# A four-layer model on one core: rows turned by transposing DMA, queries projected with keys and values

## The chip, the cores and the metric

The kernel runs on one core of a Trainium2 chip. A core has five engines with instruction streams of their own: TensorE (PE in the profile, its weight loads PEld), VectorE (DVE), ScalarE (ACT), GpSimd (POOL) and SyncE (SP). Transfers go through 16 DMA engines that they share. A transfer is issued by an engine's queue, here nearly always SP's, and a queue issues in order: an issue that waits for something holds up all those behind it. Matmul results land in PSUM, eight banks of 2 KB per partition; the other data live in SBUF.

The metric is the device time of one execution in microseconds.

## What is computed

The input is 2048 tokens of width 640 in bfloat16. Four layers follow each other, A B A B, each of the form `x = x + f(layernorm(x))`, with the same weights for both A layers and for both B layers.

Layer A is attention in four segments of 512 tokens, with 32 heads of width 20, and a linear memory carried over the segments. Per head and segment:

```
logits = q @ k.T * scale + causal mask;  a_dot = softmax(logits) @ v
a_mem  = phi(q) @ M / (phi(q) @ z + 1e-6)      # phi(t) = t + 1 for t > 0, else exp(t)
o      = g * a_mem + (1 - g) * a_dot           # g = sigmoid(beta)
M += phi(k).T @ v;   z += sum of phi(k)
```

and the heads, side by side again, are multiplied by `wo`.

Layer B works through 64 segments of 32 tokens, with 32 heads of width 128. Each segment is put behind 8 memory rows, projected to queries, keys and values, and attended with a mask; the 8 memory rows of a segment's output are the memory of the next segment. So the 64 steps of B form one chain.

## The kernel before

**Layer A.** The heads are taken in groups of four: eight groups per segment, 32 in a layer (`NGR`), numbered g. A loop over g runs two groups longer than that, since a group's work is spread over several turns: the projections for g + 1, the scores of g, the second pass over the scores for a group one to two turns back, and the product with the values for g - 2. Each turn has four slots (`half` and `ph`). In each slot PE first visits score tiles, then works off a list of other items:

- Visits: S tiles are scores of queries against keys, from which DVE takes the negative maximum of each row (`s_max`, tile a_nm). T tiles are the same product turned round, with the maximum already in the queries (tile a_q, from `q_with_max`), which ACT passes through exp into a_PT; POOL then clears what lies above the diagonal.
- Items (`SLOTS`): QP (`proj_q`: queries, already turned, width on partitions), KV0 and KV1 (`proj_kv`: keys and values in natural layout, tokens on partitions, half a segment each), KT (`k_turn`: keys turned by PE), Q2 (`q_with_max`), NUM (`state_num`: the memory's share), UP (`state_up`: the memory's update), PV, and from the finished segment before otps (`out_stage_a`: the attention rows of 128 tokens turned by PE, copied by ACT to a_oT) and YP0, YP1 (`out_stage_b`: the product with `wo`, in two halves, to which DVE adds the residual a_xr into a_xnew).
- `seg_step` loads, normalises (`seg_norm`) and turns (`seg_tr`: five PE transposes, an ACT copy to a_xnT) the rows of the next segment, at the turns and slots in `TPS`.

S and T tiles share three PSUM buffers of two banks (`psx`); all items share two buffers of one bank (`pg`), so an item must wait until the tile of the item two before it has been copied out.

PE runs in the order of the program. For ACT, DVE and POOL `KeyOrder` sorts the instructions: each has a kind, and its place is that of its slot (`K.base`) plus the lag of its kind in `A_LAGS`, in slots. So a smaller lag puts an instruction earlier on its engine, and a step that moves to another slot moves its places too. DMA issues stand in SP's queue in the order that the compiler's planner gives them.

At the end of the layer the last segment's rows are turned by PE (`last_turns`) and written out; there the normalising of layer B's first rows already begins. While the first A layer runs, the weights of B are loaded piece by piece (`side_loads`), and the padded weights of A are kept in memory (`keep_padded`) for the second A layer.

**Layer B.** A step s projects its own 32 columns with the weights as moving operand (`thin_mm`: b_Ka, b_Kb, b_Qa, b_Qb, b_Va, b_Vb), turns the results (`transp4`), takes scores, softmax and the product with the values (b_OTP), and multiplies by the output weights (b_OPS). What concerns the 24 first tokens of a segment is written at once (`store_head`); the 8 last tokens come out of the following step's memory rows and are collected in b_OTdef for four segments, multiplied later in four pieces (`od_chunk`, b_OPSd) and written by `od_end` and `tail_dma`. On the last step the columns of the step after it are zeros. When the loop is over, four pieces, an `od_end` and two stores are left.

**Joints.** Where layer B ends and A begins, A's first rows (a_xt), its weights (a_wq_pad, a_wkv) and B's last stores stand in SP's queue together.

Of the kernel before, what the change touches and what calls it, by code (L numbers as in the profile page):

```python
# [18 lines left out]
F32 = mybir.dt.float32  # L19
# [18 lines left out]
def alloc_consts(tc, ctx):  # L38
# [7 lines left out]
    C.pad = cp.tile([128, 2, 12], BF16, name="c_pad")  # L46
# [10 lines left out]
def build_consts(nc, tc, C):  # L57
    with ExitStack() as tctx:
# [13 lines left out]
        for i in range(2):  # L72
            nc.vector.tensor_copy(C.negu[:, i, :], neguf[:])
# [125 lines left out]
class AWeights:  # L199
# [3 lines left out]
A_LAGS = {"dsel": 0.5, "EK": -1.0, "EKm": 1.05, "EQ": 2.0, "Kn": 0.5, "MZ": 3.5, "MZb": 3.5, "NM1": -0.3, "On": 3.2, "adn":  # L203
# [6 lines left out]
def build_gates(nc, pool, W, A_beta):  # L210
    bb = pool.tile([128, 32], BF16, name="a_beta_bf")
    with nc.allow_non_contiguous_dma(reason="beta bcast"):
        nc.sync.dma_start(bb[:], A_beta.partition_broadcast(128))
    e = pool.tile([128, 32], F32, name="a_beta_e")
# [9 lines left out]
def load_A_weights(nc, W, A_wq, A_wk, A_wv, A_wo, padded, stage):  # L224

    first = not padded
    if first:
        for nm, src in (("wq", A_wq), ("wk", A_wk), ("wv", A_wv)):
            nc.sync.dma_start(stage[nm], src.rearrange("(c p) n -> p c n", p=128))
    else:  # L230
        nc.sync.dma_start(W.wq[:].rearrange("p c h s -> p (c h s)"), padded["wq"])
        nc.sync.dma_start(W.wkv[:].rearrange("p c g n -> p (c g n)"), padded["wkv"])
    nc.sync.dma_start(W.wo[:], A_wo.rearrange("(c p) n -> p c n", p=128))
    if first:
        K = yield
        nc.gpsimd.memset(W.wq[:, :, :, 20:32], 0.0)
        cast = K("cast").vector
        cast.tensor_copy(W.wq[:, :, :, 0:20], stage["wq"].rearrange("p c (h d) -> p c h d", d=20))
        for i, nm in enumerate(("wk", "wv")):
            cast.tensor_copy(W.wkv[:, :, :, 80 * i:80 * i + 80], stage[nm].rearrange("p c (g n) -> p c g n", n=80))  # L240
        yield


def keep_padded(nc, tc, W, padded):
    for nm, pad, n in (("wq", W.wq, 1024), ("wkv", W.wkv, 1280)):
        padded[nm] = tc.dram_tile([128, NCH * n], BF16, name=f"a_{nm}_home")
        nc.sync.dma_start(padded[nm], pad[:].rearrange("p c h s -> p (c h s)"))


def layer_A(nc, tc, C, W, x_src, x_dst, src_is_bf16, nseg=4, out_bf16=False, xb_dst=None, load_w=None, side_loads=None):  # L250
# [7 lines left out]
    with ExitStack() as ctx:  # L258
# [4 lines left out]
        W.wq = pw.tile([128, NCH, 32, 32], BF16, name="a_wq_pad")  # L263
        W.wkv = pw.tile([128, NCH, 8, 160], BF16, name="a_wkv")
# [6 lines left out]
        qp3 = pool("a_q3", 3)  # L271
# [18 lines left out]
        MZ32 = ste.tile([128, 8, 128], F32, name="a_MZ32")  # L290
        nc.vector.memset(MZ32[:], 0.0)
        MZb = stm.tile([128, 8, 128], BF16, name="a_MZb")
        vaug = [stm.tile([128, 4, 4, 32], BF16, name=f"a_vaug{i}") for i in range(4)]
        Kn = [stm.tile([128, 4, 4, 32], BF16, name=f"a_Kn{i}") for i in range(2)]
        phik = [ste.tile([128, 4, 4, 32], BF16, name=f"a_phik{i}") for i in range(2)]
        NM = [stm.tile([128, 4, 4, 32], BF16, name=f"a_NM{i}") for i in range(2)]

        def pads(i, eng):
            for on, dst, k in ((i < 2, Kn, 0), (True, vaug, 1)):
                if on:  # L300
                    src = C.pad[:, k, :].unsqueeze(1).unsqueeze(1).to_broadcast([128, 4, 4, 12])
                    (eng.copy if eng is nc.scalar else eng.tensor_copy)(dst[i][:, :, :, 20:32], src)

        nc.vector.tensor_scalar(out=MZ32[:].rearrange("p g (j e) -> p g j e", e=32)[:, :, :, 20],
                                in0=C.identb[:].rearrange("p (j e) -> p j e", e=32)[:, :, 20].unsqueeze(1).to_broadcast([128, 8, 4]),
                                scalar1=1e-6, scalar2=None, op0=ALU.mult)
# [20 lines left out]
        def seg_norm(n_, tt):  # L327
# [4 lines left out]
            for i in range(2):  # L332
                K("st").vector.bn_stats(out=stats[:, i, :], in_=xt[:, 320 * i:320 * i + 320])
# [9 lines left out]
        def seg_tr(n_, tt):  # L343
# [3 lines left out]
            xn = d["xn"][tt]  # L347
            tps = (pg if n_ else psx).tile([128, NCH, 128], BF16, name="a_tps", tag="pg" if n_ else "x")
# [4 lines left out]
        def out_stage_a(n_, tt):  # L353
# [6 lines left out]
            tps = pg.tile([128, NCH, 128], BF16, name="a_otps", tag="pg")  # L360
            for c in range(NCH):
                nc.tensor.transpose(tps[:, c, :], d["Onat"][:, tt, 128 * c:128 * c + 128], C.identb[:])
            K("oT").scalar.copy(oT[:], tps[:])

        def out_stage_b(n_, tt, halves=(0, 1)):
# [3 lines left out]
            if xr is None:  # L369
                xr = wkl.tile([128, D], BF16 if src_is_bf16 else F32, name="a_xr")  # L370
                nc.sync.dma_start(xr[:], x_src[r0:r0 + 128, :])
# [14 lines left out]
            xnb = w1l.tile([128, D], BF16, name="a_xnb")  # L386
            if n_ == nseg - 1:
                nc.scalar.copy(xnb[:], xnew[:])
            else:
                K("xnb").gpsimd.tensor_copy(xnb[:], xnew[:])  # L390
            nc.sync.dma_start(xb_dst[r0:r0 + 128, :], xnb[:])
# [3 lines left out]
        def proj_q(g):  # L395
            n, G = divmod(g, 8)
            s_ = GS[g] = {}
            xnT = SEG[n]["xnT"]
            wqG = W.wq[:, :, 4 * G:4 * G + 4, :].rearrange("p c h s -> p c (h s)")
            QP = pg.tile([128, 512], F32, name="a_QP", tag="pg")  # L400
            for c in range(NCH):
                nc.tensor.matmul(QP[:], lhsT=wqG[:, c, :], rhs=xnT[:, c, :], start=(c == 0), stop=(c == NCH - 1))
            qT = qp3.tile([128, 512], BF16, name="a_qT")
            K("qT").scalar.copy(qT[:], QP[:])
            s_["qT"] = qT
            if n >= 1:
                EQ = w1.tile([128, 512], BF16, name="a_EQ")
                K("EQ").scalar.activation(out=EQ[:], in_=qT[:], func=ACT.Exp)
                rq = w1.tile([128, 512], BF16, name="a_rq")
                K("rq").vector.tensor_scalar(out=rq[:], in0=qT[:], scalar1=0.0, scalar2=None, op0=ALU.max)  # L410
# [3 lines left out]

        def proj_kv(g, hf):
            n, G = divmod(g, 8)
            xnT = SEG[n]["xnT"]
            KV = pg.tile([128, 2, 160], F32, name="a_KV", tag="pg")
            for t2 in range(2):
                tt = 2 * hf + t2  # L420
                for c in range(NCH):
                    nc.tensor.matmul(KV[:, t2, :], lhsT=xnT[:, c, 128 * tt:128 * tt + 128], rhs=W.wkv[:, c, G, :],
                                     start=(c == 0), stop=(c == NCH - 1))
            for kd, dst, o in (("Kn", Kn[g % 2], 0), ("va", vaug[g % 4], 80)):
                K(kd).scalar.copy(dst[:, 2 * hf:2 * hf + 2, :, 0:20], KV[:, :, o:o + 80].rearrange("p t (j s) -> p t j s", s=20))
            GS[g]["va"] = vaug[g % 4]

        def k_turn(g):
            KT_ = pg.tile([128, 4, 128], BF16, name="a_KT", tag="pg")
            for tt in range(4):  # L430
                nc.tensor.transpose(KT_[:, tt, :], Kn[g % 2][:, tt, :, :].rearrange("p j s -> p (j s)"), C.identb[:])
            kT = qp4.tile([128, 512], BF16, name="a_kT")
# [956 lines left out]
```

## Time and profile before

| | us |
|---|---|
| median of 3 runs (2574.44 to 2577.28) | 2575.98 |
| the profiled execution | 2574.74 |
| its span | 2573.0 |

| engine | busy us | share of the span |
|---|---|---|
| PE | 2486.0 | 97% |
| PEld | 1639.1 | 64% |
| DVE | 1675.5 | 65% |
| ACT | 1519.1 | 59% |
| POOL | 696.2 | 27% |

The granted TensorE clock is 0.998 of full speed. The A layers lie at about 20 to 340 and 1300 to 1625 us of the span, the B layers between and behind them. PE is busy throughout; DVE and ACT are nearly full in the A layers and about half full in B. So the averages over the span are of little use, and the readings below are by stretch.

In a row of the timeline the first number is the start, the second the time from the first start to the last end of the merged instructions; since an engine overlaps an instruction with the next, what one costs is better read from its start to the start of the next. In a row of the chain of work the second number is only the part that lies on the chain. A row of waits has the total, the number and the longest.

### The profile page before, as it was taken

What the parts mean: (1) busy time and instruction counts of PE and PEld (TensorE: products, weight loads), DVE (VectorE), ACT (ScalarE), POOL (GpSimd) and SP (SyncE); (2) the same over time, 40 slices, a digit from 0 to 9 for tenths busy, and PEclk for the clock granted to TensorE, in tenths of its full rate; (3) what the DMA queues carried; (4) which work ended last, traced back from release to release, by engine and by line L of the source; (5) the groups of instructions that cost most, each with busy time, mean ns of one, the idle gap of its engine ahead of it and who ended that gap; (6) DMA issues with size and microseconds to landing.
All of it is one profiled execution on the core that took longest, in us unless ns stands there. A gap on an engine that the chain in (4) does not pass through costs nothing.

```text
span 2573.0 us, 139432 instructions
## 1 busy us (share of the span) xinstructions
PE 2486.0 (97%) x62088; PEld 1639.1 (64%) x62088; DVE 1675.5 (65%) x4597; ACT 1519.1 (59%) x3430; POOL 696.2 (27%) x1471
## 2 busy tenths in 40 slices
PE   7999999999999999999989999999999999999998
PEld 5666576666666666666655665766666666666665
DVE  8999845565556556555579998455655655555555
ACT  6999945555555545444369999445554555555443
POOL 5677621111111111111146776111111111111110
PEclk9999999999999999999999999999999999999999
DMA  4122372222222222121220212721212122111111
GB/s 158 46 85 78 91 239 45 50 48 44 51 45 48 46 50 46 39 39 29 63 84 17 68 53 86 233 47 43 45 41 50 42 45 47 42 42 34 38 26 21
DMA packets 325308, 157.18 MB, mean 61 GB/s; under 512 B 244960, under 2 KB 309600, under 8 KB 322912
## 3 DMA queue, kind: packets, MB, share of 16 engines
q1 hardware_dynamic: 324704, 148.26, 22.1%
q8 instruction: 485, 7.95, 1.3%
q14 instruction: 119, 0.97, 0.1%
HBM read 96.46 MB, written 51.71 MB: 58 GB/s over the span
## 4 chain that ended last, share of the span: by engine, by line
PE 78%; DVE 10%; ACT 8%; issue 2%; DMA 1%; POOL 1%; SPq 0%; ACTq 0%; DVEq 0%; POOLq 0%
PE b_OPS L110 11%; PE b_tail L110 6%; PE b_Ka L110 5%; PE b_Kb L110 5%; PE b_Qa L110 5%; PE b_Qb L110 5%; PE b_Va L110 5%; PE b_Vb L110 4%; DVE a_nm L139 4%; PE b_SP L110 4%; ACT a_PT L139 4%; PE b_vtail L110 3%; PE b_OPSd L110 3%; PE b_OTP L110 3%; PE a_S L110 2%
## 5 line engine op out<-in xcount | busy, mean ns | idle before, releaser
L110 PEld LDWEIGHTS <-b_HX 128*32 128x32 bf16 x15360 | 427.8, 96 | 331.3 <-issue 1.3
L110 POOL TENSOR_TENSOR b_Pn<-b_E,b_rs 128x200 bf16<-128x200 bf16 x128 | 78.0, 609 | 1332.7 <-PE b_Vb L110 1016.9
L139 DVE TENSOR_REDUCE a_nm<-a_S 128x2 f32<-128x512 f32 (+3 forms) x512 | 395.0, 816 | 53.1 <-PE a_S L110 38.1
L139 ACT ACTIVATE a_PT<-a_T 128x1024 bf16<-128x1024 f32 (+1 forms) x384 | 345.8, 904 | 28.3 <-PE a_T L110 21.0
L110 PE MATMUL b_OPS<-b_wo,b_OTsb 128*32 128x320 bf16 x8192 | 303.1, 300 | 1.6 <-issue 0.5
L110 PEld LDWEIGHTS <-b_OTsb 128*32 128x32 bf16 x8192 | 205.7, 96 | 76.3 <-DVE b_OTsb L110 3.3
L139 POOL TENSOR_SCALAR_AFFINE_SELECT a_PT<-a_PT 128x256 bf16<-128x256 bf16 x380 | 188.5, 501 | 154.7 <-ACT a_PT L139 153.4
L110 DVE CAST b_HX<-b_MT 128x8 bf16<-128x8 f32 x372 | 63.6, 172 | 234.0 <-PE b_MT L110 228.3
L110 ACT CAST b_msb<-b_OPS 128x64 bf16<-128x64 f32 x378 | 69.5, 256 | 223.7 <-PE b_OPS L110 223.6
L110 ACT CAST b_kq<-b_Kb 128x512 bf16<-128x512 f32 x128 | 74.9, 585 | 201.4 <-PE b_Kb L110 201.4
L110 DVE COPY b_KT<-b_TPak 128x128 bf16<-128x128 bf16 x128 | 28.7, 224 | 228.2 <-PE b_TPak L110 228.2
L110 DVE TENSOR_SCALAR b_kq<-b_Qa 128x512 bf16<-128x512 f32 x128 | 88.5, 691 | 120.1 <-PE b_Qa L110 116.8
L110 PE MATMUL b_Va<-b_wv,b_HX 128*32 128x512 bf16 x2520 | 161.0, 380 | 0.0
L110 PEld LDWEIGHTS <-b_kq 128*128 128x128 bf16 x2080 | 116.8, 98 | 69.4 <-ACT b_kq L110 56.4
L110 PE MATMUL b_Vb<-b_wv,b_HX 128*32 128x512 bf16 x2520 | 160.7, 379 | 0.0
L110 PE MATMUL b_Ka<-b_wk,b_HX 128*32 128x512 bf16 x2520 | 159.1, 379 | 0.1
L110 PE MATMUL b_Qb<-b_wq,b_HX 128*32 128x512 bf16 x2520 | 158.6, 379 | 0.0
L110 PE MATMUL b_Kb<-b_wk,b_HX 128*32 128x512 bf16 x2520 | 158.6, 379 | 0.0
L110 PE MATMUL b_Qa<-b_wq,b_HX 128*32 128x512 bf16 x2520 | 158.6, 379 | 0.0
L110 DVE CAST b_OTsb<-b_OTP 128x160 bf16<-128x160 f32 (+1 forms) x384 | 130.5, 376 | 38.8 <-PE b_OTP L110 34.6
L110 ACT CAST b_kq<-b_Ka 128x512 bf16<-128x512 f32 x128 | 74.9, 585 | 108.9 <-PE b_Ka L110 108.9
L110 PE MATMUL b_vtail<-b_wv,b_TX 128*32 128x256 bf16 x2880 | 133.9, 271 | 2.4 <-issue 2.3
(206 smaller groups left out, 5432.5 us busy)
## 6 DMA issues: line engine op xcount, KB each, us to landing
b_QKd<-b_tu SPq DMA_DIRECT2D x128, 128.0 KB
b_tl<-b_QKd SPq DMA_DIRECT2D x64, 256.0 KB
b_wv<-in_B_Wv_dram SPq DMA_DIRECT2D x10, 1024.0 KB
b_wo<-in_B_Wo_dram SPq DMA_DIRECT2D x16, 640.0 KB
b_Vth<-b_VTd SPq DMA_DIRECT2D x512, 16.0 KB
b_XO<-xres SPq DMA_DIRECT2D x256, 30.0 KB
b_VTd<-b_vt SPq DMA_DIRECT2D x224, 32.0 KB
b_xt<-xres_bf SPq DMA_DIRECT2D x40, 160.0 KB
```

The costliest lines, as they stand in the source:

```text
L110: r = f(*a, **k)
L139: r = f(*a, **k)
```

## The change

In layer A:

- `seg_tr` for all segments but the first, and `out_stage_a`, issue a transposing DMA from SP in place of five PE transposes and an ACT copy. The DMA of `out_stage_a` stands one turn of the loop, less one slot, ahead of the first product that reads it.
- Queries are projected together with keys and values, in natural layout, by `proj_qkv`: for half a segment ten matmuls of 240 columns and one ACT copy of 480 elements into a tile that holds queries, keys and values of four groups in turn. `qk_turn` turns keys and queries by eight PE transposes into one PSUM tile, copied by one ACT instruction of 1024 elements; the feature map of the queries starts from there. `q_with_max` now is four transposes of the natural queries, into whose free columns POOL has written the negative maxima (so POOL clears these columns first).
- The memory's update is done per head (16 matmuls of 32 columns) instead of four heads at once with a mask on DVE. DVE adds the result to the state, a quarter as wide as before, and POOL spreads it, masked, into a_MZb. In the feature map of the keys POOL now makes the part above zero from the keys themselves, next to ACT's exp instead of after it.
- Items are ordered `YP0 QKV0 | otps Q2 QKV1 NUM | KQT UP YP1 | PV`, and some lags change.

At the joints:

- The first A layer starts the normalising of its four tiles one behind the other, after the constants, and builds the gates before the loop.
- The last segment of A has four buffers for the bfloat16 rows, and loads all its residual rows before its end.
- B's last step leaves out the projection of the zero queries, multiplies the deferred rows before its own b_OTP, and takes its own last 8 rows with the others. Some of the last stores go by ACT's queue.
- For the second A layer the weights of the first two groups are one load on SP's queue and those of the other six one on ACT's queue, placed behind B's last ACT instruction.

```diff
 def load_A_weights(...):
-        nc.sync.dma_start(W.wq[:].rearrange("p c h s -> p (c h s)"), padded["wq"])
-        nc.sync.dma_start(W.wkv[:].rearrange("p c g n -> p (c g n)"), padded["wkv"])
+        home = padded["wqkv"].rearrange("p (c g n) -> p c g n", c=NCH, g=8)
+        nc.sync.dma_start(W.wqkv[:, :, 0:2, :], home[:, :, 0:2, :])
+        f = nc.scalar.dma_start(W.wqkv[:, :, 2:8, :], home[:, :, 2:8, :])
...
 def seg_tr(n_, tt):
+            if n_:
+                nc.sync.dma_start_transpose(out=d["xnT"][:, :, 128 * tt:128 * tt + 128], in_=xn[:])
+                return
...
 def out_stage_a(n_, tt):
-            tps = pg.tile([128, NCH, 128], BF16, name="a_otps", tag="pg")
-            for c in range(NCH):
-                nc.tensor.transpose(tps[:, c, :], d["Onat"][:, tt, 128 * c:128 * c + 128], C.identb[:])
-            K("oT").scalar.copy(oT[:], tps[:])
+            nc.sync.dma_start_transpose(out=oT[:], in_=d["Onat"][:, tt, :])
...
+        def proj_qkv(g, hf):
...
+            P_ = pg.tile([128, 2, 240], F32, name="a_QKVp", tag="pg")
+            for t2 in range(2):
+                tt = 2 * hf + t2
+                for c in range(NCH):
+                    nc.tensor.matmul(P_[:, t2, :], lhsT=xnT[:, c, 128 * tt:128 * tt + 128], rhs=W.wqkv[:, c, G, :],
+                                     start=(c == 0), stop=(c == NCH - 1))
+            K("Kn").scalar.copy(QKV[g % 4][:, 2 * hf:2 * hf + 2, :, 0:20], P_[:].rearrange("p t (j s) -> p t j s", s=20))
+
+        def qk_turn(g):
+            s_ = GS[g]
+            T_ = pg.tile([128, 2, 4, 128], BF16, name="a_KQT", tag="pg")
+            for i, src in enumerate((Kn[g % 4], Qn[g % 4])):
+                for tt in range(4):
+                    nc.tensor.transpose(T_[:, i, tt, :], src[:, tt, :, :].rearrange("p j s -> p (j s)"), C.identb[:])
+            kq = qp4.tile([128, 2, 512], BF16, name="a_kqT")
+            K("kT").scalar.copy(kq[:].rearrange("p a k -> p (a k)"), T_[:].rearrange("p a t k -> p (a t k)"))
...
 def state_up(g):
                 for tt in range(4):
-                    nc.tensor.matmul(UP[:], lhsT=pk[:, tt, :, :].rearrange("p j s -> p (j s)"),
-                                     rhs=va[:, tt, :, :].rearrange("p j s -> p (j s)"), start=(tt == 0), stop=(tt == 3))
-                K("upm").vector.tensor_tensor(out=upm[:], in0=UP[:], in1=C.bdmask[:], op=ALU.mult)
-                K("MZ").gpsimd.tensor_tensor(out=MZ32[:, G, :], in0=MZ32[:, G, :], in1=upm[:], op=ALU.add)
-                K("MZb").gpsimd.tensor_copy(MZb[:, G, :], MZ32[:, G, :])
+                    for j in range(4):
+                        nc.tensor.matmul(UP[32 * j:32 * j + 32, :], lhsT=pk[:, tt, j, :], rhs=va[:, tt, j, :],
+                                         start=(tt == 0), stop=(tt == 3), tile_position=(0, 32 * j), skip_group_check=True)
+                K("MZ").vector.tensor_tensor(out=MZ32[:, G, :], in0=UP[:], in1=MZ32[:, G, :], op=ALU.add)
...
 def q_with_max(g):
-            nc.tensor.matmul(Q2[:], lhsT=C.identb[:], rhs=s_["qT"][:], start=True, stop=False, skip_group_check=True)
-            for qc in range(4):
-                nc.tensor.matmul(Q2[:, 128 * qc:128 * qc + 128], lhsT=N_[:, qc, :, :].rearrange("p j s -> p (j s)"), rhs=C.identb[:],
+            for tt in range(4):
+                nc.tensor.transpose(Q2[:, tt, :], Qn[g % 4][:, tt, :, :].rearrange("p j s -> p (j s)"), C.identb[:])
...
-        SLOTS = (('otps', 'QP', 'UP'), ('Q2', 'KV0', 'NUM'), ('KV1', 'YP0'), ('KT', 'PV', 'YP1'))
+        SLOTS = (('YP0', 'QKV0'), ('otps', 'Q2', 'QKV1', 'NUM'), ('KQT', 'UP', 'YP1'), ('PV',))
...
-            no, Go = divmod(g - OUT_LAG, 8)
+            no, Go = divmod(g - OUT_LAG + (what == "otps"), 8)
...
 layer B, in a step:
+            if last:
+                nc.gpsimd.memset(QT[s][:, :, 24:32], 0.0)
+            else:
+                Qa = thin_mm(cols, W.wq, 0, "b_Qa")
+                qa = kq(Qa, "dve", SCB)
...
+            if last:
+                od_chunk()
+                oda = dict(od)
+                od_begin(s - 3, XOe, "tail")
+                for _ in range(4):
+                    od_chunk()
...
+            if last:
+                od_end(oda)
+                od_end(nm="e")
```

More of the change, by code (lines that the diff above doesn't have):

```diff
@@ L262, in layer_A @@
         pw = pool("a_w", 1)
-        W.wq = pw.tile([128, NCH, 32, 32], BF16, name="a_wq_pad")
-        W.wkv = pw.tile([128, NCH, 8, 160], BF16, name="a_wkv")
+        W.wqkv = pw.tile([128, NCH, 8, 240], BF16, name="a_wqkv")
         pxT = pool("a_xnT", 2)
@@ L393, in layer_A @@
+            if n_ == nseg - 1:
+                nc.scalar.copy(xnb, xnew[:])
+            else:
+                K("xnb").gpsimd.tensor_copy(xnb, xnew[:])
+            nc.sync.dma_start(xb_dst[r0:r0 + 128, :], xnb)
         GS = {}
-        def proj_q(g):
+        def proj_qkv(g, hf):
             n, G = divmod(g, 8)
-            s_ = GS[g] = {}
+            GS.setdefault(g, {})["va"] = vaug[g % 4]
             xnT = SEG[n]["xnT"]
[L399 to L406, printed above, removed]
+            if hf == 0 and g >= 4:
+                K("q0").gpsimd.memset(Qn[g % 4][:, :, :, 20:22], 0.0)
+            P_ = pg.tile([128, 2, 240], F32, name="a_QKVp", tag="pg")
[5 more added lines that the diff above has]
+            K("Kn").scalar.copy(QKV[g % 4][:, 2 * hf:2 * hf + 2, :, 0:20], P_[:].rearrange("p t (j s) -> p t j s", s=20))
@@ L413, in proj_q @@
                 s_["phiq"] = phiq
[L415 to L432, printed above, removed]
-            K("kT").scalar.copy(kT[:], KT_[:].rearrange("p t k -> p (t k)"))
-            GS[g]["kT"] = kT
         def phi_k(g):
@@ L451, in no_tile @@
             if step not in NOs:
[L452 removed]
+                NOs[step] = wk.tile([128, 2, 4, 4, 21], F32, name="a_no", tag="a_no")
             return NOs[step]
@@ L609, in norm @@
                 K("On").gpsimd.tensor_tensor(out=Ov, in0=s_["AD"][:, 0], in1=AD[:, 1], op=ALU.add)
+        gates = build_gates(nc, st, W, side_loads[1]) if side_loads is not None else iter(())
+        next(gates, None)
         for tt in range(4):
@@ L658, in item @@
                 state_up(g - 1)
-            elif what == "QP" and g + 1 < NGR:
-                proj_q(g + 1)
             elif what == "Q2" and 0 <= g - 1 < NGR:
@@ L669, in item @@
                 state_num(g)
-            elif what == "KT" and g + 1 < NGR:
-                k_turn(g + 1)
+            elif what == "KQT" and g + 1 < NGR:
+                qk_turn(g + 1)
             elif what == "PV" and 0 <= g - 2 < NGR:
```

169 lines of the change are left out of this document (83 added, 86 removed), and 4 rows, old and new, of the table A_LAGS.

## The prediction

> **What bounds the kernel now.** I read the table of stretches first, because the kernel is four layers, A B A B, with different limits, and an average over them says nothing. The columns are the length of the stretch and then, for PE, PEld, DVE, ACT and POOL, the busy time with its count, the granted clock, the DMA share and GB/s. These are the steady parts of the two A layers (30 of the 32 groups of each):
>
> ```profile
> 22.00:310.00 288.00, 268.64 (x3843) 173.34 (x3842) 262.79 (x469) 260.33 (x501) 201.31 (x416) 1.00 0.22 67
> 1304.00:1591.00 287.00, 267.57 (x3832) 172.80 (x3830) 262.45 (x469) 259.05 (x499) 195.94 (x371) 1.00 0.13 39
> ```
>
> PE is busy 268.6 of 288 us (93%), DVE 262.8 (91%), ACT 260.3 (90%). Three engines share the bound, and each loses 19 to 28 us to short waits on the others; DMA, at 13 to 22%, is nearly free. So work taken from PE and ACT pays only until DVE, from which the change takes almost nothing, is left as the bound. One group of four heads takes 288/30 = 9.6 us, a slot (a quarter) 2.4 us.
>
> Second the timeline of PE, for what one step costs from its start to the start of the next:
>
> ```profile
> 150.27 1.24 PE L110 MATMUL a_QP<-a_xnT,a_wq_pad 128*128 128x512 bf16 x5
> 151.35 0.39 PE L110 MATMUL a_UP<-a_vaug,a_phik 128*128 128x128 bf16 x4
> ...
> 152.36 0.39 PE L110 MATMUL a_Q<-a_qT,c_identb 128*128 128x512 bf16 x1
> ...
> 152.81 0.86 PE L110 MATMUL a_KV<-a_wkv,a_xnT 128*128 128x160 bf16 x10
> ...
> 155.00 0.86 PE L110 MATMUL a_KV<-a_wkv,a_xnT 128*128 128x160 bf16 x10
> 155.70 0.84 PE L110 MATMUL a_YP<-a_wo,a_oT 128*128 128x320 bf16 x5
> ...
> 157.14 0.40 PE L110 MATMUL a_KT<-c_identb,a_Kn 128*128 128x128 bf16 x4
> 157.37 1.15 PE L110 MATMUL a_PV<-a_vaug,a_PT 128*128 128x32 bf16 x40
> ```
>
> The query projection takes 1.08 us (five of 512 columns), ten key-and-value matmuls of 160 columns 0.70 us (70 ns each, 0.44 ns a column; the weight load is hidden), the five matmuls of Q2 0.45 us, four transposes 0.23 us. The same for ACT:
>
> ```profile
> 151.06 1.03 ACT L139 ACTIVATE a_PT<-a_T 128x1024 bf16<-128x1024 f32 x1
> 151.98 0.59 ACT L139 CAST a_qT<-a_QP 128x512 bf16<-128x512 f32 x1
> 152.44 1.06 ACT L139 ACTIVATE a_PT<-a_T 128x1024 bf16<-128x1024 f32 x1
> ...
> 154.31 0.35 ACT L139 CAST a_Kn<-a_KV 128x160 bf16<-128x160 f32 x1
> 154.48 0.38 ACT L139 CAST a_vaug<-a_KV 128x160 bf16<-128x160 f32 x1
> ```
>
> 1024 elements hold ACT 0.92 us, 512 0.46, 160 0.17: 0.9 ns an element, with little fixed cost on top. Last I read the chain around the four joints.
>
> **Steady part of A, per layer.** *Projection.* 20 matmuls of 240 columns at 0.44 ns are 2.1 us (106 ns each, so the weights stay hidden), against 1.08 + 1.40 = 2.48: -0.4 x 30 = -12 us of PE. *Q2* becomes four transposes: -0.22 x 30 = -6.6. *Turning queries with the keys* adds four: +0.23 x 30 = +6.9. *Row transposes* that go to DMA: 24 sets of five at 0.29 us (five quarters of 0.23): -7. *The state update* goes from four wide matmuls to 16 narrow ones on column tiles, as b_SP's are:
>
> ```profile
> 1273.64 0.70 PE b_SP L110 x65
> ```
>
> That is 11 ns each: 0.18 us instead of 0.23, -1 in 24 groups. The other price is a_PV's, 29 ns each (+0.23 us a group, +6). I take 11, the same form. PE in all: about -20 us, to 249.
>
> *ACT.* Before, a group's copies are 0.46 + 4 x 0.17 + 0.46 = 1.60 us. After, two of 480 elements (0.43 each) and one of 1024 (0.92) are 1.78: +0.18 x 30 = +5, against the change. The 24 row copies (640 elements, 0.59 by the same rate) leave: -14. ACT: -9, to 251. Besides, the longest wait of ACT goes with them:
>
> ```profile
> ACT a_oT L139 <- PE a_otps L110: 7.4, 9, 1.1
> ```
>
> *DVE.* The masked copy of the state goes, and an add of a quarter of its width comes:
>
> ```profile
> 151.85 0.29 DVE L139 TENSOR_TENSOR a_upm<-a_UP,c_bd 128x128 f32<-128x128 f32 x1
> ```
>
> Between nothing and all of 0.29 us; small DVE steps are mostly fixed cost, so I take -0.1 x 24 = -2, to 260.6. *POOL* loses an add, and its copy becomes a masking product; at 70% busy it sets nothing. So DVE becomes the bound, at 260.6. If it loses the same share as PE loses now (288/268.6 = 1.07), a layer's steady part takes 279: -9. One thing works against it: in the twelve groups with an output projection, the second YP now follows the 1024-wide KQT copy with only the state update between, where a_PV (1.15 us) stood before. With two PSUM buffers it waits for that copy, 0.92 less 0.2, 0.7 us, 8 us of PE a layer; PE is then at 257, still under DVE. I take **-8 a layer, -16 in two**; ends 0 (these waits eat it all) and -14 a layer (DVE at 95%).
>
> *What hides the DMA transposes.* Rows for the next segment are turned at least two groups (19 us) before use. An attention tile's transpose stands on SP's queue behind the store of the tile two before, and its reader is the first YP two groups on:
>
> ```profile
> 311.19 0.32 SPq L391 DMA_DIRECT2D xres_bf<-a_xnb  x1
> ```
>
> ```profile
> 322.65 0.85 PE L110 MATMUL a_YP<-a_wo,a_oT 128*128 128x320 bf16 x5
> ```
>
> That is 11 us from queue to use. No row shows a transposing DMA. Nearest are plain stores of the same 160 KB, from the chain at the end of the first A:
>
> ```profile
> 347.02 2.03 DMA xres_bf<-a_xnb
> ...
> 349.89 3.35 DMA xres_bf<-a_xnb
> ```
>
> At 2.0 or 3.4 us it is hidden and costs PE nothing, and I take that. If the cover were gone, each us past 11 costs 24 us over both layers. The Trainium skill ("VectorE: DVE Perf Modes", The three transpose paths) gives 1309 ns for a 128x128 block by DMA against 390 ns by TensorE; five blocks are 6.5 us, an estimate from that page, which speaks against the exchange in latency but would leave the sum as it is. SP does not wait long at them: the rows it needs are normalised one to three slots earlier.
>
> **Joints.** *A to B.* The bfloat16 copies of the last rows wait for those two stores out of their single buffer; now they have four. In the second A the last residual rows are loaded early instead of blocking DVE:
>
> ```profile
> 1626.49 4.90 DMA a_xr<-xres
> ```
>
> PE has projections of B to do meanwhile, so I take -2 and -2.5 (ends 0 and -5 each); late next is the load of the output weights.
>
> *B to A.* The last step's queries, needed by nobody, go:
>
> ```profile
> 1269.24 1.08 PE b_Qa L110 x20
> ```
>
> Two halves, each 1.08 us and four transposes (0.23): 2.6 us. The greater part is the load of the key-and-value weights, held on SP's queue behind a store that waits for DVE:
>
> ```profile
> 1288.15 0.48 DVE b_XOe L110
> ...
> 1290.38 0.62 SPq L1071
> ...
> 1291.05 7.21 DMA a_wkv<-a_wkv_home
> ```
>
> ```profile
> 1298.31 2.85 PE L110 MATMUL a_KV<-a_wkv,a_xnT 128*128 128x160 bf16 x20 [4.31 <-DMA a_wkv<-a_wkv_home]
> ```
>
> Now the first two heads' groups come in a small load of their own, the rest and that store go by ACT's queue, and the six DVE additions for B's outputs (0.48 each as in the first row) are brought forward. 4.3 us of wait, 2.6 of queries and, as some of the additions stood beside other waits, 2 of their 2.9: -9, ends 0 (SP's order still holds the small load back) and -12. Late next is the normalising chain on DVE. The Trainium skill ("DMA: Bandwidth & Descriptors", Issuing engines are not separate DMA queues) says that another issuing engine saves only the time to issue; by that the 4.3 us would stay and the sum be 2545. The row shows a transfer not yet issued, which this rule does not cover.
>
> *The end.* Before, after the last OPS:
>
> ```profile
> 2563.75 3.00 PE L110 MATMUL b_OPSd<-b_wo,b_OTdef 128*32 128x320 bf16 x72
> ...
> 2566.38 2.17 DMA out_dram<-b_xnbd
> ```
>
> Of these 72 deferred matmuls 64 (2.7 us) move ahead of the last OTP, where PE waits for the softmax, and the wait for that store goes. They overfill the gap there by about 2 us, which the missing queries pay. I take -5 (ends -2, -7). *The start* gains nothing: all three weight casts must now be done before the first projection. 0 (+1, -2).
>
> **Sum.** -16 - 2 - 2.5 - 9 - 5 = -34.5 against the profiled 2574.74, 2540; that run lies 1.2 us under the median 2575.98, so **2541**.
>
> **Rivals.**
> *Joints only.* DVE holds the A layers where they are: the gain is 18.5 us, 2557. For: DVE loses only 2 us of work. Against: its idle time is mostly waits for PE.
> *Transposes land late* (the other side). One mechanism, at the first YP of each of 24 output tiles. From 11 us to landing PE stops; at 11 + 34/24 = 12.4 us the gain is gone; at 16 us, five times the slower plain store, the time is 2541 + 24 x 5 = 2661. Against: 3.35 us is far off. For: no row shows this kind of transfer.
> *The feature map of the queries comes late.* It starts from the joint turn in slot 2 instead of slot 0, so ACT and DVE have three slots (7.2 us) instead of five before a_NUM needs it, on two queues that are 90% full. Each us late costs 24 a layer; at 1 us both layers lose 48, 2589. It decides from 0.7 us.
> *Nothing moves:* the terms sit at their zero ends, 2576.
> *More:* all far ends, about 2518.
>
> **Chances.** Forecast 0.57 (own range 2522 to 2550), joints only 0.20, late transposes 0.08, late feature map 0.08, nothing 0.03, more 0.04. 0.2% is 5 us, about what this measurement can tell from no change. Faster 0.57 + 0.20 + 0.04 = 0.81, within 0.03, slower 0.16. The range 2512 to 2585 leaves out the late transposes and most of the late feature map.
>
> **What would show it.** Steady stretches of about 279 us with PE near 250 busy and DVE the fullest; no waits of a_YP on DMA; a KV-type wait after the second weight load gone and the first scores of the second A some 9 us sooner after B's last values; no a_xnb or a_xr waits; last OPS to end about 4.5 us. Wrong would be: a_YP or the projection waiting for a_oT or a_xnT, a_NUM waiting for a_phiq, ACT fuller than before, or SP stuck ahead of the weights again.

## The result, and the profile after

The changed kernel takes 2610.43 us (median of four runs, 2608.60 to 2611.85). The kernel before, run beside it, takes 2575.93. The ratio is 1.0134, with a 95% interval of 1.0116 to 1.0151: it is 34.5 us slower, where 35 us less were forecast. The profiled execution has a span of 2606.8 us against 2573.0, and its mean granted clock is 0.977 against 0.998.

I split both spans at the same events: the first scores of an A layer, the first filler matmul (a_W) of its tail, the first b_Ka of a B step, and the b_Ka on b_HXz (the zero columns) in the last B step. All times are in us. The last column adds up to the difference of the spans but for rounding.

| stage | before | after | forecast | measured change |
|---|---|---|---|---|
| start to first scores | 20.5 | 20.4 | 0 | -0.1 |
| first A, scores to its tail | 305.7 | 321.6 | -8 | **+15.9** |
| first A's tail to B's first step | 57.1 | 64.2 | -2 | **+7.1** |
| first B's steps | 884.7 | 884.2 | 0 | -0.5 |
| last step of B to scores of the second A | 34.6 | 29.0 | -9 | -5.6 |
| second A, scores to its tail | 305.9 | 321.6 | -8 | **+15.7** |
| second A's tail to B's first step | 56.0 | 63.5 | -2.5 | **+7.5** |
| second B's steps | 886.6 | 884.1 | 0 | -2.5 |
| end | 22.0 | 18.2 | -5 | -3.8 |

So the loss lies in the two A layers and in the two joints behind them. The stretches of the steady parts answer to the first two lines shown of before (same columns):

```profile
22.00:310.00 288.00, 254.63 (x3747) 168.30 (x3744) 251.19 (x448) 238.88 (x368) 196.13 (x407) 0.92 0.27 75
1304.00:1591.00 287.00, 248.85 (x3661) 165.34 (x3662) 247.76 (x450) 229.28 (x355) 184.62 (x350) 0.93 0.22 63
```

All three busy engines are emptier than before (PE 88% and 87%, DVE 87% and 86%, ACT 83% and 80%), so none of them is the bound. And the granted clock is 0.92 and 0.93, where it was 1.00. Two things are to be explained: what PE waits for, and why its clock falls.

The waits of PE from 22 to 310 us, first of the kernel before, then of the changed one (total us, times, longest):

```profile
PE a_T L110 <- ACT a_PT L139: 1.9, 7, 0.3
PE a_T L110 <- DVE a_nm L139: 2.8, 9, 0.4
```

```profile
PE a_T L110 <- ACT a_PT L139: 10.5, 19, 0.8
PE a_YP L110 <- DVE a_MZ L139: 8.5, 8, 1.1
PE a_T L110 <- DVE a_nm L139: 5.2, 15, 0.4
PE a_NUM L110 <- ACT a_q L139: 1.1, 6, 0.2
```

The first row is new in its size, the second altogether. No row names a transposing DMA. The first one can be watched in a single group without an output projection (a light group). PE and then ACT, from the timeline of the changed kernel:

```profile
101.95 0.39 PE L110 MATMUL a_T<-a_q,a_kqT 32*128 32x512 bf16 x2
...
102.37 0.62 PE L110 MATMUL a_KQT<-c_identb,a_QKV 128*128 128x128 bf16 x8
102.92 0.28 PE L110 MATMUL a_UP<-a_QKV,a_phik 128*32 128x32 bf16 x16
...
104.14 0.39 PE L110 MATMUL a_T<-a_q,a_kqT 32*128 32x128 bf16 x4 [0.30 <-DVE a_nm L139]
105.02 0.28 PE L110 MATMUL a_T<-a_q,a_kqT 32*128 32x256 bf16 x2 [0.48 <-ACT a_PT L139]
```

```profile
103.03 1.01 ACT L139 COPY a_kqT<-a_KQT 128x1024 bf16<-128x1024 bf16 x1 [0.41 <-PE a_KQT L110]
103.94 2.44 ACT L139 ACTIVATE a_PT<-a_T 128x1024 bf16<-128x1024 f32 x3
```

The scores a_T of slot 2 stand ready from about 102.3. ACT does not take them: the KQT copy has a smaller key in the order written out by hand (2.3 + 0.1 = 2.4, the exponential 2.0 + 0.5 = 2.5). ACT first waits 0.41 us for PE to turn keys and queries, then copies for 0.91 us, and only then turns to the exponential. The third round of a_T needs the tile which that exponential frees, and PE stands. In the kernel before the turn was in slot 3 and its copy had the key 3.4, behind the wide exponential of that slot (3.0 + 0.2 = 3.2):

```profile
69.67 1.02 ACT L139 ACTIVATE a_PT<-a_T 128x1024 bf16<-128x1024 f32 x1
70.59 0.58 ACT L139 COPY a_kT<-a_KT 128x512 bf16<-128x512 bf16 x1
```

What this does to the clock is in four stretches of 3.41 us (length, PE busy, granted clock, DMA share, GB/s):

```profile
99.66:103.07 3.41, 3.38 (x56) 1.00 0.00 0
103.07:106.48 3.41, 2.63 (x70) 1.00 0.20 69
106.48:109.89 3.41, 3.27 (x20) 0.50 0.05 15
109.90:113.31 3.41, 3.23 (x44) 1.00 0.43 91
```

In the second PE is busy 2.63 of 3.41 us. In the third the clock is half, and only 20 matmuls start. The steady parts hold twelve such stretches in each A layer, 3.41 us long (one is 6.83), many of them 10.24 us apart (106.48, 116.72, 126.96). The kernel before shows none there.

Last the joint. The issue of B's first rows on SP's queue, before and after:

```profile
329.81 0.66 SPq L860 DMA_DIRECT2D b_xt<-xres_bf  x1
...
342.29 0.32 SPq L385 DMA_DIRECT2D xres<-a_xnew  x1
```

```profile
362.51 0.32 SPq L391 DMA_DIRECT2D xres_bf<-a_Onat  x1
362.92 0.67 SPq L847 DMA_DIRECT2D b_xt<-xres_bf  x1
...
368.49 0.72 PE L110 MATMUL b_lntps<-c_identb,b_xt 128*128 128x128 bf16 x5 [7.29 <-DVE b_xt L110]
```

Before, the loads went out 12 us ahead of A's last stores. After, they stand behind all of them, and PE has nothing for 7.3 and another 1.6 us. Behind that gap the clock is at half for 10.24 us (length, PE busy, granted clock, DMA share, GB/s), which it was not at this joint before:

```profile
362.49:365.90 3.41, 0.00 (x0) 1.00 0.70 241
365.90:376.14 10.24, 6.03 (x56) 0.50 0.88 298
```

### The profile page after: what moved, and what is told of

Its sections match the earlier page's. It is cut to its first block, busy times and chain, and to the rows that moved or that the text cites. A ratio compares the mean times of both kernels' runs of the same rounds, so it can differ in the third digit from the quotient of the medians.

```text
span 2606.8 us, 139581 instructions
## 1 busy us (share of the span) xinstructions
PE 2478.2 (95%) x62200; PEld 1646.0 (63%) x62200; DVE 1678.2 (64%) x4593; ACT 1502.7 (58%) x3190; POOL 698.9 (27%) x1484
## 4 chain that ended last, share of the span: by engine, by line
PE 80%; DVE 13%; ACT 4%; issue 2%; DMA 1%; POOL 0%; SPq 0%; DVEq 0%; ACTq 0%; POOLq 0%
PE b_OPS L110 11%; PE b_tail L110 6%; DVE a_nm L139 6%; PE b_Ka L110 5%; PE b_Kb L110 5%; PE b_Qa L110 5%; PE b_Qb L110 5%; PE b_Va L110 5%; PE b_Vb L110 4%; PE b_SP L110 4%; PE a_QKVp L110 3%; PE b_vtail L110 3%; PE b_OPSd L110 3%; PE a_S L110 3%; PE b_OTP L110 3%; ACT a_PT L139 2%
## 5 line engine op out<-in xcount | busy, mean ns | idle before, releaser
L139 ACT ACTIVATE a_PT<-a_T 128x1024 bf16<-128x1024 f32 (+1 forms) x384 | 327.0, 888 | 29.3 <-PE a_T L110 21.1
L110 PE MATMUL a_QKVp<-a_wqkv,a_xnT 128*128 128x240 bf16 x1280 | 170.6, 287 | 4.5 <-DVE a_wqkv L139 2.5
L110 PE MATMUL a_T<-a_q,a_kqT 32*128 32x512 bf16 (+3 forms) x1024 | 131.5, 311 | 35.9 <-ACT a_PT L139 24.3
```

Of the source, the lines that this page charges most:

```text
L110: r = f(*a, **k)
L139: r = f(*a, **k)
```

## The experiments

Each run is compared with runs of the kernel before on the same chip. Those had medians of 2576.7 us (the first four runs), 2580.2 (the next four) and 2581.7 (the last two), so ratios are compared across the three sets.

**Is it the transposing DMA?** First the turn is undone in the changed kernel:

```
-            if n_:
-                nc.sync.dma_start_transpose(out=d["xnT"][...], in_=xn[:])
-                return
...
-            nc.sync.dma_start_transpose(out=oT[:], in_=d["Onat"][:, tt, :])
+            (five PE transposes into a_otps, copied by K("oT").scalar)
```

> Undoes one part alone: the normalised rows and the attention rows are turned by TensorE and copied by ScalarE again, all else as in the changed kernel (2610). Theory (the transposing DMA is innocent; the A layers lose because PE now stands still about 0.8 us in each light group, and its clock is then halved for 3.4 us): the turns add 24 x 0.29 = 7 us of PE and 24 x 0.59 = 14 us of ScalarE to a layer, the clock still falls in most of the light groups (8 or more stretches at half clock in a layer), each A layer stays at 315 to 330 us from first scores to its tail, 2600 to 2635 in all. Rival (the transposing DMA costs the time, by its latency, its traffic or SP's queue): the A layers fall back to 308 or less, 2585 or less in all.

Measured: 2637.8 us, ratio 1.0241 (1.0225 to 1.0258), a little above the expected range and far from the rival's. The A layers take 336.1 and 334.4 us, 14.5 and 12.8 more than in the changed kernel, also above their range. PE's waits now name the copies and the turns that came back:

```profile
PE a_QKVp L110 <- ACT a_oT L139: 6.8, 9, 1.0
PE a_tps L110 <- DVE a_MZ L139: 6.4, 7, 1.1
```

Then the other direction: the kernel before with this one part of the change, the same two calls of dma_start_transpose in its own seg_tr and out_stage_a.

> The kernel before with one part of the change alone: the rows of segments 1 to 3 and the attention rows are turned by transposing DMA, projections and everything else as before (2576). Theory (the DMA turn is harmless and takes 24 x 0.29 us of PE and 24 x 0.59 us of ScalarE out of a layer): the wait of a_oT on a_otps goes, no wait on the transposes, clock stays 1.00 because the other work of PE is untouched; A layers 2 to 8 us shorter each, 2560 to 2574. Rival (the DMA turn costs, by SP's queue or by taking PE's work away so that the clock falls here too): 2585 or more.

Measured: 2558.5 us, ratio 0.9913 (0.9899 to 0.9928), just below the expected range. The A layers take 298.0 and 299.5 us, 7.7 and 6.4 less than before. The DMA turn is a gain in both surroundings, and the rival is out. The rest of the change costs more than this gives.

**Is it the clock?** Useless matmuls are put into the light groups of the changed kernel:

```
-            for e in range(2):
+            light = not ((g - OUT_LAG) // 8 >= 1 and (g - OUT_LAG) % 8 < 4)
+            for e in [0, 1] * (4 if light and pr == 1 and r == 1 else 1):
                 nc.tensor.matmul(X[:, e, m0:m1], lhsT=C.identb[:], ...
```

> The changed kernel with useless work on PE: in each group without an output projection (20 of 32 in a layer) the two mask matmuls of the round of scores in the last slot are issued four times instead of once, 3 x 0.21 = 0.64 us a group; what they write is overwritten by the last pair. Theory (the clock gate): with the idle time filled the granted clock stays at 1.00, the 12 half-clock stretches of a layer go (up to 1.7 us each), light groups come from 10.2 to 10.5 down to 9 to 9.5 us, an A layer from 321.6 to about 308, 2580 to 2590 in all: more work, less time. Rival 1 (the half clock is only a sign; what holds a group is the chain through ScalarE and DVE): the time does not move, 2605 to 2615. Rival 2 (PE's work is the bound): 20 x 0.64 x 2 = 26 us more, 2636.

Measured: 2592.6 us, ratio 1.0067 (1.0047 to 1.0086), 18 us less with some 13 us of PE work more in each A layer. The theory had expected a little more gain (2580 to 2590); the rivals would have had 2605 and over. The wait for the exponential is as large as in the changed kernel, and the clock is full (a wait of PE from 22 to 310 us, then the stretch from 22 to 130, columns as above):

```profile
PE a_T L110 <- ACT a_PT L139: 10.4, 25, 0.5
```

```profile
22.00:130.00 108.00, 97.98 (x1479) 66.87 (x1478) 97.23 (x175) 88.44 (x135) 68.81 (x157) 1.00 0.24 66
```

The same stretch of the changed kernel has 97.26 us of PE, at a clock of 0.86. The A layers fall by 7.5 and 8.4 us. So the half clock is a cost of its own, of about 8 us a layer, and not only a sign. That is half of the loss; the wait is still there.

**Is it the place of the copy?** One number:

```
-A_LAGS = {... "kT": 0.1, ...
+A_LAGS = {... "kT": 0.3, ...
```

> One number changed: the place of the 1024-wide copy of turned keys and queries (KQT) in ScalarE's order, from just before the exponential of slot 2 (key 2.4) to just behind it (2.6; that exponential has 2.5). Theory (this 0.9 us copy, standing ahead of the exponential that frees PE's score tile, makes the 0.8 us wait in each light group, and this wait is what lets the clock fall): the wait of a_T on a_PT falls from 10.5 us to under 4, the half-clock stretches go, light groups take 8.6 to 9.3 us instead of 10.2 to 10.5, an A layer 300 to 310 instead of 321.6, 2575 to 2595 in all. Rival 1 (PE simply has too little work for its clock): idle time of the same size at another wait, clock as before, 2605 to 2615. Rival 2 (the copy, now later, holds up the scores of the next group or YP1): slower, 2620 or more.

Measured: 2568.8 us (nine runs), ratio 0.9970 (0.9957 to 0.9983), below the kernel before and below the expected range. ACT in a light group, then PE's wait from 22 to 310 us:

```profile
93.60 1.05 ACT L139 ACTIVATE a_PT<-a_T 128x1024 bf16<-128x1024 f32 x1
94.52 1.04 ACT L139 COPY a_kqT<-a_KQT 128x1024 bf16<-128x1024 bf16 x1
```

```profile
PE a_T L110 <- ACT a_PT L139: 0.2, 1, 0.2
```

The exponential comes first, the wait is gone, and so are nearly all stretches at half clock (one is left from 22 to 310 us). The length of a light group is read between the starts of two KQT; first the changed kernel, then this run:

```profile
62.21 0.64 PE L110 MATMUL a_KQT<-c_identb,a_QKV 128*128 128x128 bf16 x8
72.36 0.64 PE L110 MATMUL a_KQT<-c_identb,a_QKV 128*128 128x128 bf16 x8
```

```profile
60.51 0.64 PE L110 MATMUL a_KQT<-c_identb,a_QKV 128*128 128x128 bf16 x8
68.61 0.64 PE L110 MATMUL a_KQT<-c_identb,a_QKV 128*128 128x128 bf16 x8
```

10.15 us against 8.10. The A layers are 302.0 and 299.8 us, 19.6 and 21.8 less than in the changed kernel and 4 to 6 less than before. So this one key made up the whole loss of the A layers, and a little more.

**The wait of the second YP.** On top of the last run:

```
-SLOTS = (..., ('KQT', 'UP', 'YP1'), ('PV',))
+SLOTS = (..., ('KQT', 'YP1'), ('UP', 'PV'))
```

> The run with the KQT copy behind the exponential (2569), and besides the state update moved from slot 2, between KQT and the second YP, to slot 3, ahead of a_PV. Theory (in the eight groups of a layer that have both, YP1 stands 1.0 us because the PSUM buffer it needs is freed by a_MZ, which DVE takes only after its two maxes of the slot, 1.8 us): the wait a_YP on a_MZ, 8.7 us in a layer, falls below 2, these groups come from 10.9 to 11.4 us down to about 10.2, 4 to 7 us a layer, 2555 to 2562 in all. Rival (the wait only moves on, to a_PV or to the next a_Q, as DVE is full in these groups): 2565 to 2572.

Measured: 2556.5 us, ratio 0.9907 (0.9892 to 0.9921). The wait of a_YP on a_MZ, which had been 8.7 us with the copy already moved, no longer stands among PE's waits. The second A falls by 10.1 us, the first by 2.1. The two layers differ in their clock as well: it is at half in four stretches of the first A (two in the run before this step) and in none of the second (two). Some of the wait did move on, as the rival had it: to the score tiles (a_S on a_nm, 5.2 to 8.2 us) and a little to Q2, which needs the buffer of the first YP (6.6 us before this step):

```profile
PE a_Q L110 <- DVE a_xnew L139: 7.5, 9, 1.2
```

**The joint A to B.** The addresses that the program gives its pools in SBUF suggest why the loads are late. The pool of B's first row tiles (b_x, 5.9 KB) lay, in the kernel before, over a_EK, a_qT and the first a_kT buffer, which A is done with early. In the changed kernel it lies over two of the four a_kqT buffers and the first a_PT buffer, which also holds a_xnew to the end: the joint weights tile is 3.8 KB smaller than the two it replaces, a_MZ32 3 KB, and the a_qT pool is gone, so everything behind them has moved down. First the pool alone was moved, in the changed kernel:

```
+        bx = pool("b_x", 1)
         W.wv = pool("b_wv", 1).tile([128, NCH, 4096], BF16, name="b_wv")
...
-        bx = pool("b_x", 1)
```

> Only the place in SBUF of layer B's four small row tiles is changed: their pool is allocated ahead of B's value weights, where it lies over the projection weights of A, instead of over the four kqT buffers and a PT buffer that A reads to its end. Theory (the loads of B's first rows wait for those buffers, so they stand on SP's queue behind the last stores of A, and PE has nothing to do for 8 us at each A to B joint): the loads are issued before the last stores, the time from A's tail to B's first steps falls from 64.2 and 63.5 to about 56 each; the B to A joint may lose up to 3 us because the weight load there now waits for the row tiles; 2592 to 2602 in all. Rival (the joint is held by the last stores or the last DVE adds of A, not by these loads): joints as before, 2608 to 2613.

Measured: 2609.0 us, ratio 1.0130 (1.0112 to 1.0147), no gain; the sum is where the rival put it. Yet the loads went out early, and the joints are 2.8 and 2.4 us shorter (61.4 and 61.1). Two other waits took the place of the old one. DVE's statistics of B's rows waited for the last x store, since their own tile lay over a_xnew (from the chain of this run). And at the B to A joint (37.1 us instead of 29.0) the projection weights of the second A waited for the moved pool (from PE's timeline):

```profile
356.50 3.12 DMA xres<-a_xnew
...
359.72 0.90 DVE b_ln_st L110 x2
```

```profile
1314.97 4.18 PE L110 MATMUL a_QKVp<-a_wqkv,a_xnT 128*128 128x240 bf16 x20 [6.50 <-DMA a_wqkv<-a_wqkv_home]
```

Then all of it was cleared, on top of the moved copy: small A pools that are free early (a_wk1 with a_EQ and a_rq, and a new a_wk1b with a_xnb alone) go under B's row tiles, a_EK is made wider by 896 bytes as a pad, and b_x goes ahead of b_hx.

```
-        qp4 = pool("a_q4", 4)
-        up = pool("a_unit", 3)
-        wk = pool("a_wk", 2)
         w1 = pool("a_wk1", 1)
+        w1b = pool("a_wk1b", 1)
+        qp4 = pool("a_q4", 4)
+        up = pool("a_unit", 3)
+        wk = pool("a_wk", 2)
...
+        bx = pool("b_x", 1)
         hp = pool("b_hx", 3)
```

> The run with the KQT copy behind the exponential (2569), and besides only places in SBUF: the pools of A that are free early (feature map of queries, bfloat16 rows) now lie under the pool of B's first row tiles, which itself moves ahead of B's other small pools. In the run that put this pool over the projection weights the loads went out early and only 2.8 and 2.4 us came back, as DVE's statistics still waited for the last x stores (their tile lay over a_xnew), and the B to A joint lost 8. Theory (places in SBUF alone set the joint): loads and memory rows go out ahead of the last stores, DVE's statistics no longer wait for a store, A's tail to B's first step falls from 64.6 and 63.2 to 55 to 58, the B to A joint stays at about 30; 2552 to 2560. Rival (the four row stores or PE's eight YPs in a row hold the joint): 61 or more each, 2563 to 2570.

Measured: 2549.2 us, ratio 0.9886 (0.9869 to 0.9903), just below the expected range. The joints are 53.2 and 57.1 us, 11.4 and 6.1 less, and B to A stays at 29.3. The first of B's loads, the first of A's last stores, and PE among the last YPs:

```profile
328.81 0.67 SPq L848 DMA_DIRECT2D b_xt<-xres_bf  x1
...
339.00 0.34 SPq L381 DMA_DIRECT2D xres<-a_xnew  x1
```

```profile
340.49 0.28 PE L110 MATMUL b_lntps<-c_identb,b_xt 128*128 128x128 bf16 x2
340.60 1.52 PE L110 MATMUL a_YP<-a_wo,a_oT 128*128 128x320 bf16 x10
```

PE turns B's rows between A's last matmuls, as it did before (from 341.92 us on there). The long stretch at half clock behind the first A is gone too: the 160 matmuls of b_tail that follow take 9.10 us, where they took 11.39. Only places in SBUF were changed (and, with the pad, the row length of a_EK), so they made the joint.

**All together.** The three repairs, and the residual add of YP earlier on DVE ("xnew" from 0.6 to 0.0) for the wait that was left at Q2:

> The three changes together (KQT copy behind the exponential, state update in slot 3, row tiles clear), and the residual add of YP taken earlier on DVE (0.0 instead of 0.6 after its slot begins), because after the first of these a_Q waits 6.6 us in a layer for a_xnew. If the steps are independent: 2569 - 10 - 13 - up to 8, 2538 to 2550. If DVE is the bound in the groups with an output projection, the earlier add delays the maxes instead and the sum is 2548 to 2560.

Measured: 2530.8 us, ratio 0.9809 (0.9794 to 0.9824): 49 us below the kernel before, and the best of all. That is below both expected ranges: by their ratios the moved update and the cleared tiles had given about 16 and 22 us, where 10 and 13 had been put in. A layers 296.2 and 287.7, joints 53.1 and 55.8. The second A:

```profile
1290.00:1570.00 280.00, 262.49 (x4068) 179.47 (x4067) 266.83 (x486) 256.60 (x403) 206.91 (x391) 1.00 0.25 68
```

DVE is 95% full, more than PE (94%) and ACT (92%). Without the early add:

> The run with all changes (2531), but the residual add of YP at its old place on DVE. If the steps add up (copy 2569, joints -20, state update -13): about 2535, the early add then worth 4 us, and the wait of a_Q on a_xnew is back at 4 to 7 us a layer. Rival (the early add does most of it): 2540 or more. Rival (nothing): 2530.

Measured: 2540.7 us, ratio 0.9838 (0.9821 to 0.9855), 0.3% above the run with it. The spans differ by 6.1 us, of which 3.2 and 2.2 lie in the A layers (299.4 and 289.9), and the wait that the early add removes is back: a_Q on a_xnew, 7.6 us in the first A against 1.9. The median lies just inside the rival's range, since the early add is worth more than the 4 us expected. In ratios the steps do add up: 0.9970, less 0.0063 for the update and 0.0084 for the tiles, is 0.9823, within the interval of this run. And with the rows turned by PE in the best version:

> The run with all changes (2531), but the normalised rows and the attention rows turned by TensorE and copied by ScalarE. Theory (the DMA turn is a plain gain, about 18 us in the kernel before): the 7 us of PE and 14 us of ScalarE come back in each layer where DVE, at 95%, is already nearly full, so 2545 to 2565. Rival (DVE alone is the bound now, and the turns hide beside it): 2531 to 2538.

Measured: 2569.7 us, ratio 0.9952 (0.9936 to 0.9969), above both expected ranges. So DVE is not the only bound. A layers 311.9 and 306.8: the DMA turn is worth 15.7 and 19.1 us a layer here, more than the forecast's terms for it (7 us of PE, 14 of ACT). The largest wait of PE (22 to 300 us) says where from: two PSUM buffers are now shared by more steps, and the copy out of one of them is waited for.

```profile
PE a_QKVp L110 <- ACT a_oT L139: 8.4, 10, 1.0
```

## Why the prediction was wrong

**Steady part of A: wrong, +15.9 and +15.7 for -8.** The step that failed is the one on ACT. It counted the KQT copy as throughput ("+0.18 x 30 = +5, against the change") and did not ask what the moved copy is moved past. The turn went from slot 3 to slot 2, and with its old lag of 0.1 its copy passed the exponential of that slot. The order of ACT was in the code before the change; two keys, 2.4 and 2.5, would have shown it. With the copy behind the exponential the layers take 302.0 and 299.8 us, -3.7 and -6.1 against before: near the term, and inside its ends.

**The sizes on PE were right but for a few tenths.** From start to start in the group shown, the eight transposes of KQT take 0.55 us (0.46 forecast) and the state update 0.21 (0.18). The feared second price of the update, 29 ns a matmul, did not come. The sum over them was somewhat too large: in the second A of the best version, at full clock, PE is busy 269.8 us from first scores to tail, against 285.0 before, 15 less and not 20.

**That less work on PE can only help: wrong, and nowhere stated.** The sum took a clock of 1.00 as given, since the steady parts before show nothing else. The filled groups show some 8 us a layer for the clock.

**The second YP: place and size right, cause wrong.** 0.7 us was forecast, for the KQT copy; 1.0 to 1.1 us came, eight times a layer, and it was a_MZ, behind DVE's maxes of 1.8 us. The run with the moved copy shows it, PE, ACT and DVE:

```profile
227.29 0.84 PE L110 MATMUL a_YP<-a_wo,a_oT 128*128 128x320 bf16 x5 [1.04 <-DVE a_MZ L139]
226.49 1.01 ACT L139 COPY a_kqT<-a_KQT 128x1024 bf16<-128x1024 bf16 x1
227.06 0.18 DVE L139 TENSOR_TENSOR a_MZ<-a_UP,a_MZ 128x32 f32<-128x32 f32 x1
```

The YP starts while the copy still runs, and right behind a_MZ. The two buffers are not taken strictly in turn: in the changed program this YP lies in the bank of the update, and KQT in the other. In the changed kernel itself the copy mostly ends only 0.14 us ahead of a_MZ, so it was luck that the forecast size came near. "Still under DVE" was wrong as well: DVE stood at 87%, so each such wait was paid.

**DVE becomes the bound: wrong for this kernel, half right for the repaired one.** In its second A DVE is the fullest engine (95%), and the layer takes 287.7 us, less than the 297.9 that the term gave. But with the rows back on PE the layers get 15.7 and 19.1 us longer with no work added on DVE, so DVE alone does not set the time.

**The transposes are hidden: right.** No wait names them, and the DMA turn alone gives 0.9% in the kernel before. The rival of the late transposes and that of the late feature map fall (a_NUM waits 1.1 us from 22 to 310, and for a_q).

**A to B: wrong, +7.1 and +7.5 for -2 and -2.5.** The single x buffers did go, as the step said. It failed in naming what PE has to do meanwhile: that work needs rows that were loaded early before, and the step did not ask where the new and smaller tiles put B's. PE stood for 7.3 and 1.6 us instead, and the 10.24 us at half clock came on top. Cleared, the joints stand at 53 to 57, -3.9 and +1.1 against before.

**B to A: right in kind, too large (-5.6 for -9).** The wait on the key-and-value weights is gone. Late next is the last x store and its reload, and then the normalising chain, all in the chain of the changed kernel:

```profile
1291.71 2.12 DMA xres<-b_XO
1293.85 0.67 SPq L1104
...
1297.01 4.27 DMA a_xt<-xres
1301.30 0.90 DVE a_ln_st L139 x2
```

L1104 is the load of the last step's x rows. It waits on SP's queue for that store, now comes in two parts for each half (four issues, 2.9 us), and A's reload stands behind it. The term counted the order of the weights on SP, and not this one. The second B's steps came out 2.5 us shorter; that was not followed up.

**The end: -3.8 for -5**, inside its ends. **The start: -0.1 for 0.**

All rivals named before missed as well. The two mechanisms that decided, an order on ACT and an address in SBUF, were not among them.

## What to carry to other kernels

When a step moves to another slot, read the order of every engine that handles its result, and put its keys beside those of its new neighbours: one copy of 0.9 us ahead of one exponential cost 40 us in a kernel of 2600. When tiles become smaller or larger, look at what the next stage allocates over them; loads that are early only because their place is free become late without any line of them having changed. And where one part of a change gains and another loses, do each alone: the DMA turn was worth 0.9% all along.

## What the runs showed of the hardware

**The clock falls without any long gap.** PE was never idle for longer than 0.85 us in the light groups; stretches of 3.41 us in which it was busy 72 to 77% of the time (once 63%) were followed by 3.4 us at half clock. The Trainium skill ("TensorE: Matmul & The Clock Gate", What's actually happening) gives a free-running window of 3413 ns, and the distances fit: 10.24 us is three of them. Its table lets the clock fall after an idle window. The joint behind the first A agrees, with PE idle from 361.20 to 368.49 us and the clock at half from 365.90; the light groups do not, as no such window stands in them. The page's section on a second HAM failure mode, psum-queue depth-cycling, speaks of micro-idles that make the clock oscillate, and that agrees. The light group had come to about 10.2 us, three windows, and so each one could meet the same window with the same pause. That this kept the state going is argued, not shown.

**Busy time alone does not decide it.** In the first of these stretches, in a group with an output projection, PE is less busy than in nearly all of those, and the next one is at full clock:

```profile
154.27:157.68 3.41, 2.37 (x45) 1.00 0.00 0
157.68:161.09 3.41, 3.25 (x68) 1.00 0.79 189
```

The same holds in a light group: from 92.83 to 96.24 us PE is busy 2.58 of 3.41 us, and the clock stays full. What it goes by stays open.

**A transposing DMA holds its queue.** On SP's queue each one takes 1.2 us to issue (least, median and most, in ns), a plain store 0.32:

```profile
L361 SPq DMA_TRANSPOSE a_oT<-a_Onat x24: 1201/1207/1875, 129.0 to 1620.3; - x24
...
L391 SPq DMA_DIRECT2D xres_bf<-a_Onat x8: 319/320/742, 358.2 to 1661.5; - x8
```

SP has room for it here. The trace does not show when they land, only that the first YP, 9.1 us after the start of the issue at the least, does not wait. The 1309 ns a 128x128 block that the Trainium skill gives ("VectorE: DVE Perf Modes", The three transpose paths) would be 6.5 us for five, an estimate from that page, and nothing here contradicts it.
